# Attention with chunk selection and a gated MLP on one core: the k operands copied straight out of PSUM

## The chip, the core and the metric

The kernel runs on one core of a Trainium2 chip. The metric is the device time of one execution in microseconds (us). TensorE (PE in the profile), VectorE (DVE), ScalarE (ACT), GpSimd (POOL) and SyncE (SP) each work through an instruction list of their own, in order. DMA queues move data; here GpSimd issues the loads and SyncE the transposing transfers, the stores and, in the kernel before, some copies from one place of SBUF to another.

## What is computed

Attention for 4 batches of 8 heads with 768 tokens and 64 numbers to a head. A query sees its own and earlier tokens, and only those in the 6 best of 24 chunks of 32 keys; a chunk's worth is bounded from the minimum and the maximum of its keys. A gated MLP over the heads' joined output follows.

```python
def _attn_ref(q, k, v):
    k_chunks = k.reshape(B, H, nc, chunk, D)
    k_min = np.min(k_chunks, axis=3)
    k_max = np.max(k_chunks, axis=3)
    ub = np.sum(np.maximum(q[:, :, :, None, :] * k_min[:, :, None, :, :],
                           q[:, :, :, None, :] * k_max[:, :, None, :, :]), axis=-1)
    ub = np.where(causal, ub, -1000000000.0)
    top_chunks = np.argsort(ub, axis=-1)[..., -top_k:]
    scores = scale * np.matmul(q, k.transpose(0, 1, 3, 2))
    mask = sel & (pos[:, None] >= pos[None, :])
    scores = np.where(mask, scores, -1000000000.0)
    attn = softmax(scores)
    return np.matmul(attn, v)

def _moe_ref(x, w_in, w_spatial, b_spatial, w_out):
    h = np.maximum(x @ w_in, 0.0)
    u, v = (h[..., :d_ff // 2], h[..., d_ff // 2:])
    v_n = (v - mean(v)) / np.sqrt(var(v) + 1e-06)
    v_s = np.einsum('ts,bsd->btd', w_spatial, v_n) + b_spatial[None, :, None]
    return (u * v_s) @ w_out
```

## The kernel before

**Tiling.** The 32 heads are taken as 16 pairs, numbered 0 to 15, four to a batch. The two heads of a pair lie side by side on the 128 partitions (64 each). All matmul operands are f16. The MLP of a batch (v, u, s and o matmuls, in six blocks of 128 tokens) can begin when the four pairs of that batch are done, and is woven between the attention of later pairs.

**A pair.** `kT` transposes k on TensorE into one PSUM buffer of the pool `ps_ml` (L680), which has three buffers and is shared with every matmul of the MLP. VectorE reads that buffer twice, for `kmax` and `kmin` (L704), and forms the chunk bounds `kb`. `qT`, `rq` and `ub` give the bounds of each query, `top` and `sel` mark the chunks left out, and `aT`/`ac` (pairs 1 to 7) or the transposing transfer `aTd` (pairs 8 to 15, L826) make the other operand, a, of the scores. The stationary operand of the scores, `kh`, is one SBUF tile for each head, in a ring of four pairs: 64 of its partitions hold the chunk indicators (written once), and the other 64 hold the head's k. The step `kop` writes those 64 partitions, which lie in the opposite half to where they stand in the transposed k. Then `sc` multiplies (three PSUM buffers), ScalarE takes the exponential (`ex`, L842), `tri` on GpSimd cuts the diagonal, `av` accumulates in the single PSUM buffer `acc` (L859), `rc` and `nm` (L869) normalise out of it, and `x` brings the result across for the MLP.

**How kop is done.** For pairs 0 to 7 VectorE or ScalarE copies each half out of PSUM (L740). For pairs 8 to 15 there are three steps: one copy `kc` of the whole transposed k into SBUF by VectorE or ScalarE (L726), which together with the two reductions releases the PSUM buffer, and two transfers on SyncE's queue from that copy into `kh` (L738).

**Order.** Nothing is scheduled by the framework. A planner written in Python (`build`, `Sim`) searched an order beforehand, and the result stands in the file as the string `ORDER`, which names every step; each engine works through its own steps in that order. `PLAN` holds the parameters. Those that count here: `kcp` is the first pair whose k is copied to SBUF first, `flip` names the steps that go to the other engine of VectorE and ScalarE than the default, and `dum` is the number of dummy matmuls (`dm0` and on) that stand between the first steps. The rule in the planner and the step in the kernel:

```python
kd=i>=p['kdma']; kc=not kd and i>=p['kcp']
...
if (kd or kc) and p['kcdma'] and i>=p['kdm']:
    op(f'kop{i}{hi}','SP',.5,deps=[kt],acq=[('kh',i)],uses=[kr],...)
else:
    ke='ACT' if i<2 else 'DVE'
...
dst, src = self.kh[hi][d0:d1], getattr(self, "kTb", self.kT)[s0:s1]
if engine == "SP":
    nc.sync.dma_start(out=dst, in_=src)
else:
    copier(engine)(dst, src)
```

Of the kernel before, what the change touches and what calls it, by code (L numbers as in the profile page):

```python
# [390 lines left out]
PLAN = {'late': 40, 'mlp_first': 8, 'qbuf': 5, 'kbuf': 6, 'vbuf': 6, 'dum': 64, 'warm0': 5.3, 'kcp': 8, 'flip': ['ac10', 'ac41', 'ac51', 'ac60', 'ac71', 'gd34', 'kc10', 'kc12', 'kc13', 'kc9', 'kh00', 'kh11', 'kop00', 'kop40', 'kop71', 'oc01', 'oc03', 'oc13', 'oc21'], 'gp': ((3, 4), (3, 5)), 'lm': 0.2, 'lm2': 1.2, 'tm': 0.8, 'dum0': 42, 'split': 1, 'rpool': (4,), 'ract': (1,)}  # L391

ORDER = """
dz id0 dm ring3 lk010 ring2 ring1 lk000 ring0 lq010 small id1 lq000 expand lk001 kh00 kh30 kh11 lk011 kT0 kh21 mlat
dm0 kTb0 lq011 kmin0 dm1 dm2 dm3 dm4 dm5 kop01 dm6 dm7 dm8 dm9 dm10 dm11 lq001 kmax0 qTb0 kh31 qT0 dm12 lk11 dm13 dm14
dm15 dm16 kb0 dm17 dm18 dm19 rq00 dm20 rq01 dm21 dm22 dm23 dm24 dm25 dm26 kop00 dm27 dm28 dm29 dm30 lk10 kh20 kT1 ub0
kmax1 kTb1 kh01 lv0 dm31 dm32 dm33 dm34 dm35 dm36 dm37 dm38 dm39 top00 dm40 dm41 kop11 dm42 qT1 kmin1 lq10 dm43 dm44
dm45 kop10 dm46 dm47 dm48 dm49 dm50 dm51 dm52 dm53 selA0 dm54 top01 kh10 mtri aTA00 dm55 kb1 dm56 dm57 dm58 sel0 rq11
lq11 aTB0 dm59 rq10 dm60 dm61 dm62 dm63 acA00 ub1 wsp0 acB0 sc000 top10 win00 sc001 ex000 aTA01 top11 sc002 lk20 ex001
acA01 sc005 kT2 sel1 ex002 sc004 kop20 lk21 ex005 sc013 ex004 sc011 kmin2 ex013 aT10 lq20 sc003 ex011 sc010 ac10 av000  # L400
ex003 kop21 aT11 lq21 ex010 sc015 av001 sc100 kmax2 ex015 av002 ac11 lv1 sc012 rc00 kb2 ex012 qT2 nm00 sc102 ex100
rq21 kT3 lk31 ex102 av010 rq20 sc014 kmax3 sc112 ex014 win21 ub2 sc101 ex112 kmin3 win11 sc104 qT3 ex101 sc111 top20
av011 ex104 sc105 av012 kb3 lk30 ex111 top21 sc103 rc01 ex105 sel2 sc113 ex103 rq31 aT20 ex113 rq30 sc115 wsp4 sc114
ac20 nm01 ub3 kop30 av100 ex114 sc201 top30 av101 ex115 win01 ex201 sc203 kop31 av102 sc110 ex203 top31 aT21 ex110
rc10 lv2 sel3 kT4 ac21 nm10 qT4 sc200 kmin4 sc205 sc202 ex200 aT30 kmax4 ex202 sc215 av110 ex205 ex215 av111 rq40
kop40 sc211 wsp5 av112 kb4 rq41 sc204 sc212 ex211 rc11 kop41 ub4 aT31 ac30 sc210 top40 lq30 kT5 ex204 nm11 xp0 ex212
top41 lq31 av200 kop50 ac31 sc213 av201 sel4 ex210 av202 win30 sc214 kmax5 qT5 ex213 sc300 ex214 xp1 rc20 win20 rq51
sc301 ex300 sc310 nm20 ex301 rq50 av210 win31 ex310 kmin5 sc311 av211 sc303 ex311 win10 sc302 x1 av212 ex303 sc304
kop51 aT40 ex302 rc21 ex304 kb5 kT6 nm21 sc305 ac40 sc315 sc313 kmin6 av300 ex305 aT41 ex315 ex313 x0 sc404 wsp1 sc312
ac41 ex404 sc314 av301 kmax6 ex312 ub5 lk40 sc401 ex314 av302 sc400 top50 xp2 ex401 rc30 sc403 top51 ex400 sc402 wsp2  # L410
sel5 ex403 nm30 aT50 ring4 ex402 sc415 kop61 av310 ac50 av311 x2 sc412 ex415 av312 kop60 sc405 qT6 ex412 lq40 sc411
ex405 kT7 rc31 ex411 nm31 sc501 sc413 tri40 rq61 ex501 sc414 xp3 rq60 ex413 kmax7 wsp3 aT51 ex414 av400 sc502 kb6
sc410 kop71 x3 sc500 av401 ac51 v00.0 ex410 kmin7 av402 ex502 v00.2 tri41 ub6 ex500 kop70 sc504 sc503 lq41 sc505 top60
ex503 v02.0 top61 v04.0 ex504 lk41 rc40 v02.2 sel6 va00 nm40 sc510 qT7 va02 lk51 v04.2 ex510 rq71 sc513 kb7 av410 rq70
ex513 lq61 v01.0 bs02 av411 ex505 aT60 va04 bs00 v01.2 tri50 av412 ac60 sc514 va01 v03.0 lv3 rc41 vs02 nm41 sc603 ub7
ex603 bs01 v03.2 x4 sc511 ex514 lb top70 wsT0 ex511 av500 vs01 top71 sc512 lv4 va03 sc515 av501 sel7 wsT1 ex515 wsc0
sc600 ex512 av502 vs00 aT61 wsc1 ex600 v05.0 lq50 rc50 ac61 nm50 kT8 sc601 v05.2 kmax8 lq51 ex601 aT70 va05 sc604
kmin8 av510 lk61 ac70 sc613 sc602 u01.0 kc8 ex604 tri51 qT8 bs05 ex613 av511 wsT2 lk50 ex602 kb8 u01.2 rq80 sc611 rq81
u00.0 ex611 bs03 sc610 aT71 ua01 wsc2 av512 u00.2 ex610 vs05 bs04 sc704 wsT5 ua00 u02.0 vs04 ex704 ac71 wsT4 vs03 rc51
u02.2 rs0 nm51 sc605 sc614 wsc5 ub8 ex605 x5 ex614 sc612 wsc4 tri60 av600 ua02 sc700 vn00 av601 wsT3 ex612 vn04 sc701  # L420
ex700 u04.0 top80 av602 wsc3 sc703 u03.0 vn01 ex703 sc615 u04.2 rc60 ex701 nm60 u03.2 ua04 u05.0 top81 ua03 av610 sel8
sc702 vn03 ex615 sc710 aTd8 kT9 ex702 vn02 tri61 sc712 ex710 av611 kmin9 s00.0 lk60 ex712 u05.2 kop80 kmax9 av612
kop81 sc715 sc705 ua05 s00.2 wout1 rc61 ex715 qT9 vn05 kc9 sc711 s01.0 nm61 ex705 sc714 kop91 kb9 s00.4 rq91 tri70 x6
av700 rq90 s01.2 gt00 sc713 s02.0 ex713 gd00 av701 ub9 ex714 kT10 top90 s01.4 ex711 kop90 s02.2 top91 tri71 sc802 sel9
sc800 gt01 sc801 ex802 aTd9 av702 wout3 s02.4 ex801 rc70 wout2 s03.0 nm70 ex800 sc804 gt02 qT10 ex804 av710 kmax10
gd01 sc803 sc805 av711 sc810 ex803 s04.0 kmin10 ex805 av712 ex810 gd02 sc815 s03.2 tri80 ex815 rc71 sc812 kb10 kc10
nm71 s03.4 wout0 s04.2 ex812 x7 gt03 lv7 kT11 sc813 rq100 av800 ex813 sc811 rq101 gd03 av801 s05.0 kmax11 ex811 sc814
av802 s05.2 ex814 kop101 rc80 kmin11 s04.4 sc905 sc901 ub10 ex905 nm80 ex901 sc904 s05.4 kb11 gt04 ex904 sc900 av810
ex900 kc11 sc911 sc903 o01.0 ex911 top100 sc915 o00.0 top101 ex915 ex903 sc902 sel10 av811 o01.2 ex902 gt05 aTd10 qT11
sc910 oc01 tri90 v10.0 rq110 o00.2 tri81 kop100 rq111 sc914 v10.2 oc00 gd04 v11.0 lq60 ex914 ub11 ex910 av812 v11.2  # L430
gd05 lv5 va10 rc81 o02.0 nm81 va11 v13.0 top110 o02.2 kop110 top111 lq71 v14.0 sel11 oc02 sc912 bs10 av900 ex912 sc913
kT12 ex913 aTd11 v13.2 kmax12 v14.2 tri91 va13 av901 sc1000 kmin12 va14 sc1002 lk71 av902 ex1000 sc1012 v12.0 rc90
ex1002 nm90 o03.0 lk70 ex1012 bs11 sc1004 sc1005 av910 ex1004 bs14 qT12 av911 ex1005 o03.2 kc12 vs14 vs11 v12.2 oc03
sc1010 kop121 v15.0 va12 rq121 x8 av912 sc1003 sc1001 rc91 bs12 u10.0 ex1001 v15.2 rq120 os02 ex1010 u11.0 nm91 kop120
va15 u10.2 vs10 kop111 bs13 av1000 ua10 u11.2 os01 bs15 o04.0 ex1003 x9 kb12 kT13 ua11 vs13 tri100 o04.2 kmax13 sc1015
sc1014 oc04 sc1013 av1001 ub12 vs12 ex1014 kmin13 av1002 o05.0 ex1015 ex1013 sc1101 top120 u12.0 kc13 vs15 sc1011
rc100 top121 sc1104 ex1101 o05.2 kop130 sel12 ex1011 u13.0 nm100 os00 qT13 ex1104 kop131 tri101 u12.2 rq131 rs1 sc1100
aTd12 av1010 oc05 lv6 vn10 sc1103 sc1102 ua12 vn11 u13.2 ex1103 vn13 av1011 u14.0 ua13 vn14 u15.0 ex1100 rq130 av1012
u14.2 kb13 ex1102 rc101 vn15 u15.2 ua14 vn12 s10.0 ua15 sc1114 ub13 s10.2 top130 sc1110 sc1105 s10.4 nm101 ex1105
ex1110 s11.0 tri110 gt10 kT14 ex1114 s11.2 kmin14 lq70 gd10 s12.0 av1100 kmax14 sc1115 s11.4 ex1115 s12.2 gt11 sc1113  # L440
av1101 s12.4 kc14 gd11 sc1112 s14.0 gt12 ex1112 sc1111 av1102 top131 ex1113 s13.0 gd12 rc110 sel13 ex1111 s15.0 nm110
s14.2 tri111 sc1203 aTd13 sc1200 s14.4 ex1203 av1110 ex1200 gt14 s13.2 x10 av1111 sc1213 av1112 sc1201 ex1213 kT15
rc111 nm111 sc1202 s13.4 kmax15 ex1202 x11 sc1205 s15.2 ex1201 qT14 gt13 s15.4 ex1205 sc1215 kc15 sc1204 o10.0 ex1204
rq140 sc1210 kop151 av1200 gt15 ex1215 o10.2 os05 tri120 av1201 kb14 os03 rq141 sc1212 oc10 sc1302 kmin15 o12.0 gd13
ex1210 av1202 ex1212 ub14 rc120 sc1300 nm120 o12.2 gd15 ex1300 top140 sc1214 v21.0 ex1302 top141 v20.0 oc12 sel14
sc1310 ex1214 v21.2 sc1211 ex1310 qT15 sc1313 aTd14 ex1211 sc1303 rq150 v20.2 va21 rq151 tri121 av1210 ex1313 kb15
o11.0 gd14 ex1303 ub15 v23.0 va20 top150 av1211 sc1314 kop150 top151 sc1311 av1212 ex1314 bs20 o11.2 kop140 ex1311
# [21 lines left out]
def kernel(  # L469
# [20 lines left out]
    prm = dict(DEF)  # L490
    prm.update(PLAN)

# [395 lines left out]

    engine = {o.name: o.eng for o in build(PLAN).order}

# [201 lines left out]
```

## Time and profile before

| what | value |
|---|---|
| median of 4 runs | 204.28 us (202.27 to 205.67) |
| profiled execution, its own time | 202.27 us |
| its span, first to last instruction | 200.6 us |
| TensorE busy | 190.6 us (95%) |
| VectorE busy | 157.4 us (78%) |
| ScalarE busy | 149.0 us (74%) |
| GpSimd busy | 80.8 us (40%) |
| data moved by DMA | 28.60 MB |
| transfers kh<-kT | 16 of 96.0 KB |
| granted TensorE clock | 1.000 |

The profiled execution is one of the four runs, the fastest. Its span leaves out 1.67 us that lie around it (202.27 less 200.6), and it stands 2.01 us under the median. A matmul's busy time in the profile runs from its start to its modelled end, and matmuls overlap, so a busy TensorE is read from the spacing of matmuls rather than from the sum of their durations.

### The profile page before, as it was taken

Reading aid. Unit: us, or ns where it says so; the run is one execution under the profiler, and the core shown is the slowest. Engines: PE = TensorE matmul, PEld = TensorE weight load, DVE = VectorE, ACT = ScalarE, POOL = GpSimd, SP = SyncE. Lnnn points to the kernel's source line nnn. Section 1 sums busy time; section 2 is a strip of 40 time slices with the busy share of each in tenths; the row PEclk is TensorE's granted clock in tenths of the full one; section 3 lists DMA queues with packets and bytes.
Section 4 is the critical chain, followed back from the end, with each engine's and each line's share of the span. In section 5 each row is a group of like instructions: output and inputs, shape, how many; then the busy total and the mean of one; then the engine's idle time right before and its main releaser. Section 6 shows DMA issues by size and latency. Waiting matters only on the chain.

```text
span 200.6 us, 5309 instructions
## 1 busy us (share of the span) xinstructions
PE 190.6 (95%) x2057; PEld 120.9 (60%) x2057; DVE 157.4 (78%) x475; ACT 149.0 (74%) x296; POOL 80.8 (40%) x97
## 2 busy tenths in 40 slices
PE   7789789999999999999999999999999999999992
PEld 7777668767677756565566555656555555444451
DVE  6899799999999999899698899797378337257430
ACT  5969799999989986777888963689899751664151
POOL 7999957452899233453751412011212130000000
PEclk9999999999999999999999999999999999999999
DMA  6999999999699999999999999988672265342335
GB/s 40 98 122 163 164 161 182 170 194 82 64 141 135 151 122 164 175 166 159 140 140 164 235 180 161 182 215 116 211 120 39 78 121 149 115 179 85 78 128 212
DMA packets 114761, 28.60 MB, mean 143 GB/s; under 512 B 108720, under 2 KB 111280, under 8 KB 114736
## 3 DMA queue, kind: packets, MB, share of 16 engines
q0 software_dynamic: 76544, 12.20, 91.2%
q1 hardware_dynamic: 38192, 16.06, 40.6%
q8 instruction: 16, 0.26, 0.6%
q14 instruction: 9, 0.07, 0.1%
HBM read 24.38 MB, written 6.29 MB: 153 GB/s over the span
## 4 chain that ended last, share of the span: by engine, by line
PE 65%; DVE 12%; DMA 11%; POOL 6%; ACT 2%; issue 2%; SPq 1%; POOLq 0%; DVEq 0%; ACTq 0%
PE mlp L957 38%; PE sc L833 12%; PE acc L859 7%; DMA xT<-x 4%; DMA qs<-in_q_dram 3%; DMA kh<-kT 2%; DVE vn L994 2%; DVE kmm L704 2%; POOL k L619 2%; PE trq L745 2%; PE tra L820 1%; POOL qs L619 1%; DVE max L775 1%; DVE x L869 1%; PE kTp L680 1%
## 5 line engine op out<-in xcount | busy, mean ns | idle before, releaser
L842 ACT ACTIVATE e<-sc 128x512 f16<-128x512 f32 (+1 forms) x192 | 93.8, 561 | 20.0 <-PE sc L833 16.3
L833 PE MATMUL sc<-a,kh 128*128 128x512 f16 (+3 forms) x256 | 61.2, 305 | 0.6 <-DMA kh<-kT 0.3
L957 PE MATMUL mlp<-w_in_sb,xT 128*128 128x512 f16 x192 | 52.2, 379 | 0.0
L848 POOL TENSOR_SCALAR_AFFINE_SELECT e<-e 128x768 f16<-128x768 f16 x24 | 21.0, 877 | 75.9 <-ACT e L842 64.6
L859 PEld LDWEIGHTS <-e 128*128 128x128 f16 x672 | 31.4, 97 | 14.8 <-DVE x L869 0.9
L957 PE MATMUL mlp<-vn,wsT 128*128 128x512 f16 x144 | 38.8, 379 | 0.4 <-DVE vn L994 0.4
L859 PE MATMUL acc<-vt,e 128*128 128x65 f16 x672 | 35.8, 193 | 0.1
L704 DVE TENSOR_REDUCE kmm<-kTp 128x24 f16<-128x768 f16 x32 | 29.7, 948 | 1.9 <-PE kTp L680 1.9
L833 PEld LDWEIGHTS <-kh 128*128 128x128 f16 x256 | 22.6, 97 | 12.8 <-DMA kh<-kT 0.8
L957 PE MATMUL mlp<-w_out_sb,gT 128*128 128x512 f16 x92 | 26.1, 379 | 0.0
L957 PEld LDWEIGHTS <-xT 128*128 128x128 f16 x192 | 17.2, 97 | 14.4 <-issue 0.2
L1000 DVE SCALAR_TENSOR_TENSOR g<-mlp,b_col,u 128x512 f16<-128x512 f32 x24 | 17.9, 747 | 9.4 <-PE mlp L957 7.4
L1020 ACT COPY o<-mlp 128x512 f32<-128x512 f32 x19 | 11.1, 589 | 16.9 <-PE mlp L957 16.5
L979 DVE BATCH_NORM_STATS2 stats<-vraw 128x6 f32<-128x512 f32 x24 | 15.9, 678 | 5.8 <-ACT vraw L974 5.8
L957 PEld LDWEIGHTS <-wsT 128*128 128x128 f16 x144 | 12.7, 97 | 10.6 <-issue 0.4
L869 DVE TENSOR_TENSOR x<-acc,rec 128x384 f16<-128x384 f32 x32 | 17.7, 552 | 1.3 <-DMA xT<-x 0.8
L989 ACT ACTIVATE u<-mlp 128x512 f16<-128x512 f32 x24 | 14.0, 597 | 4.8 <-PE mlp L957 4.1
L775 DVE MAX8 max<-ub 128x8 f32<-128x8 f32 (+4 forms) x160 | 15.3, 167 | 1.0 <-PE ub L765 1.0
L974 ACT ACTIVATE vraw<-mlp 128x512 f32<-128x512 f32 x24 | 14.1, 606 | 2.4 <-PE mlp L957 2.4
L604 POOL DMA_DIRECT2D k<-in_k_dram x14 | 14.6, 1053 | 0.5 <-DMA ws_raw<-in_moe_w_spatial_dram 0.4
L610 POOL DMA_DIRECT2D qs<-in_q_dram x14 | 14.5, 1045 | 0.7 <-DMA k<-in_k_dram 0.7
L994 DVE TENSOR_SCALAR vn<-vraw,mv,rstd 128x512 f16<-128x512 f32 x24 | 13.7, 627 | 0.8 <-ACT rstd L1030 0.6
(85 smaller groups left out, 234.1 us busy)
## 6 DMA issues: line engine op xcount, KB each, us to landing
out_dram<-o SPq DMA_DIRECT2D x23, 256.0 KB, 2.3
vt<-in_v_dram POOLq DMA_DIRECT2D x8, 384.0 KB, 9.8
k<-in_k_dram POOLq DMA_DIRECT2D x14, 192.0 KB, 7.6
qs<-in_q_dram POOLq DMA_DIRECT2D x14, 192.0 KB, 7.7
kh<-kT SPq DMA_DIRECT2D x16, 96.0 KB, 4.9
ws_raw<-in_moe_w_spatial_dram POOLq DMA_DIRECT2D x6, 192.0 KB, 6.7
w_in_sb<-in_moe_w_in_dram POOLq DMA_DIRECT2D x8, 128.0 KB, 8.5
w_out_sb<-in_moe_w_out_dram POOLq DMA_DIRECT2D x4, 128.0 KB, 3.7
```

What stands on the lines that cost most here:

```text
L604: nc.gpsimd.dma_start(out=k_tile(g)[:, :, :, hi, :].rearrange("p x t d -> p (x t) d"), in_=source(k, b, 2 * hp + 2 * hi, 2))
L704: nc.vector.tensor_reduce(self.kmm[:, m, :], src, axis=AX.X, op=op, negate=(m == 1))
L775: nc.vector.max(self.max8[:, qi - 1, hi, :], self.ub[:, c0:c0 + CPT * (qi + 1)])
L833: mm(sc[:, col:col + n], lhsT=self.kh[hi][:, t * P:(t + 1) * P], rhs=self.a[:, q0 // P:(q0 + n) // P, hi, :], start=True, stop=not diag)
L842: nc.scalar.activation(out=self.e[hi][:, g * 512:g * 512 + width], in_=self.sc[hi, g][:, 0:width], func=Act.Exp, scale=scale)
L848: nc.gpsimd.affine_select(out=blk, in_=blk, compare_op=Alu.is_ge, fill=0.0, base=0, channel_multiplier=-1, pattern=[[0, NQT], [1, P]])
L859: mm(self.av[hi][:, qi, :], lhsT=self.e[hi][:, c:c + P], rhs=self.v[hi][:, t, 0:D + 1], start=first and n == 0, stop=last and n == len(blo ...
L869: nc.vector.tensor_tensor(self.x16[:, :, hi, :], in0=self.av[hi][:, :, 0:D], in1=self.rec[hi].to_broadcast([P, NQT, D]), op=Alu.mult)
L957: mm(st[kind, ti], lhsT=lhsT, rhs=rhs, start=(j == 0), stop=(j == n - 1))
L979: nc.vector.bn_stats(st["stats", ti], st["vraw"][:, ti, :])
L994: nc.vector.tensor_scalar(vn[:, ti, :], in0=st["vraw"][:, ti, :], scalar1=st["mv"][:, ti, 0:1], scalar2=st["rstd"][:, ti, :], op0=Alu.subt ...
L1000: nc.vector.scalar_tensor_tensor(g, in0=st["s", ti], scalar=b_col[:, ti:ti + 1], in1=st["u"][:, ti, :], op0=Alu.add, op1=Alu.mult)
```

## The change

`kcp` goes from 8 to 99, so no pair has a `kc` step any more. The two `kop` steps of pairs 8 to 15 are the copies that pairs 0 to 7 had already: 64 partitions by 768 numbers out of the PSUM buffer of the transposed k into `kh`, on VectorE or ScalarE. The tile kT in SBUF, its eight copies and the sixteen transfers on SyncE's queue are gone. The PSUM buffer of a pair's transposed k is then released by four readers, two reductions and two copies, in place of three. The order was searched anew, with another `flip` list, and 50 dummy matmuls in place of 64. All other functions of the kernel are as they were.

```diff
-PLAN = {..., 'dum': 64, 'warm0': 5.3, 'kcp': 8, 'flip': ['ac10', 'ac41', 'ac51', 'ac60', 'ac71', 'gd34', 'kc10', 'kc12', 'kc13', 'kc9', 'kh00', 'kh11', 'kop00', 'kop40', 'kop71', 'oc01', 'oc03', 'oc13', 'oc21'], ...}
+PLAN = {..., 'dum': 50, 'warm0': 5.3, 'kcp': 99, 'flip': ['ac11', 'ac20', 'ac31', 'ac40', 'ac41', 'ac51', 'ac70', 'ac71', 'kc10', 'kc11', 'kc8', 'kc9', 'kh01', 'kh21', 'kh31', 'kop100', 'kop101', 'kop110', 'kop111', 'kop120', 'kop141', 'kop150', 'kop31', 'kop40', 'kop50', 'kop51', 'kop71', 'kop81', 'kop90', 'kop91', 'oc10', 'oc11', 'oc12', 'oc13', 'oc14', 'oc15'], ...}
 ORDER = """
-dz id0 dm ring3 lk010 ring2 ring1 lk000 ring0 lq010 small id1 lq000 expand lk001 kh00 kh30 kh11 lk011 kT0 kh21 mlat
-dm0 kTb0 lq011 kmin0 dm1 dm2 dm3 dm4 dm5 kop01 dm6 dm7 dm8 dm9 dm10 dm11 lq001 kmax0 qTb0 kh31 qT0 dm12 lk11 dm13 dm14
...
-lq11 aTB0 dm59 rq10 dm60 dm61 dm62 dm63 acA00 ub1 wsp0 acB0 sc000 top10 win00 sc001 ex000 aTA01 top11 sc002 lk20 ex001
-acA01 sc005 kT2 sel1 ex002 sc004 kop20 lk21 ex005 sc013 ex004 sc011 kmin2 ex013 aT10 lq20 sc003 ex011 sc010 ac10 av000
...
-u02.2 rs0 nm51 sc605 sc614 wsc5 ub8 ex605 x5 ex614 sc612 wsc4 tri60 av600 ua02 sc700 vn00 av601 wsT3 ex612 vn04 sc701
...
-kop81 sc715 sc705 ua05 s00.2 wout1 rc61 ex715 qT9 vn05 kc9 sc711 s01.0 nm61 ex705 sc714 kop91 kb9 s00.4 rq91 tri70 x6
...
+dz id0 dm small lk000 ring2 ring1 lk010 ring0 lq000 ring3 id1 lq010 expand lk011 kh01 kh00 kh31 lk001 kT0 kh11 lq011
+dm0 kTb0 kh30 kmin0 dm1 dm2 dm3 dm4 dm5 dm6 lq001 dm7 dm8 dm9 dm10 dm11 kop00 kmax0 qTb0 mlat qT0 dm12 lk10 dm13 rq01
...
+acA01 lb sc001 top10 sc005 kT2 ex001 sc002 win00 top11 ex005 sc004 sel1 ex002 win30 sc013 kmax2 aT10 ex004 lk21 sc010
...
+sc604 u01.2 ex704 rq80 sc703 ex604 rc51 kb8 aT71 nm51 sc700 ex703 sc614 tri60 ac71 av600 rs0 sc702 kop80 av601 ua01
+ub8 av602 vn04 ex700 wsT2 rc60 ex614 nm60 sc701 wsT4 ex702 top80 tri61 av610 ex701 sc713 top81 sc712 kop81 av611 lk60
...
+ex715 kT9 ua03 tri71 u05.2 kmin9 s00.0 ua05 av701 s00.2 kmax9 s01.0 s00.4 rq91 kop90 s01.2 kb9 gt00 ub9 kop91 s01.4
+top90 gd00 av702 sc801 top91 sc802 sc805 ex801 s02.0 rc70 sel9 kT10 ex802 gt01 aTd9 sc800 ex805 s02.2 nm70 ex800 sc810
...
```

How many steps of each kind stand on an engine, before and after (kinds that do not change are left out):

| step | engine | before | after |
|---|---|---|---|
| kc, whole k to SBUF | VectorE / ScalarE | 4 / 4 | 0 / 0 |
| kop, pairs 8 to 15 | VectorE / ScalarE / SyncE | 0 / 0 / 16 | 6 / 10 / 0 |
| kop, pairs 0 to 7 | VectorE / ScalarE | 11 / 5 | 7 / 9 |
| ac, copy of a | VectorE / ScalarE | 5 / 9 | 8 / 6 |
| oc, copy of the output | VectorE / ScalarE | 4 / 20 | 6 / 18 |
| gd34, copy of the gate | VectorE / ScalarE | 0 / 1 | 1 / 0 |
| kh, indicators | VectorE / ScalarE | 2 / 6 | 3 / 5 |
| dm0 and on, dummy matmuls | TensorE | 64 | 50 |

## The prediction

> **What bounds the kernel now.** I read the busy time by stage first, then the waits, then the rows of the operations that the change removes or adds. I cut the stages where the work changes: 50.4 us is the first v matmul of the MLP, and 193.7 us the end of the o matmuls.
>
> ```profile
> core 0: us, PE busy (x) PEld busy (x) DVE busy (x) ACT busy (x) POOL busy (x), PEclk, DMA share, GB/s
> 0.00:50.40 50.40, 45.06 (x683) 36.45 (x684) 46.43 (x157) 44.30 (x81) 36.71 (x50) 1.00 1.73 138
> 50.40:75.00 24.60, 24.60 (x308) 16.76 (x307) 23.96 (x81) 22.31 (x47) 16.51 (x17) 1.00 2.06 121
> 75.00:120.00 45.00, 44.29 (x467) 26.55 (x466) 39.66 (x122) 34.94 (x73) 18.45 (x21) 1.00 1.69 169
> 120.00:165.00 45.00, 44.95 (x432) 25.89 (x429) 30.83 (x85) 33.81 (x72) 9.11 (x11) 1.00 0.82 140
> 165.00:193.70 28.70, 28.70 (x160) 13.55 (x157) 15.64 (x31) 11.27 (x22) 0.00 (x0) 1.00 0.39 120
> ```
>
> From 50.4 us on TensorE has 0.76 us without work in 143.3 (0.71 and 0.05). Its busy time counts modelled ends, so I set it against spacings. The chain of waits has the last MLP block back to back:
>
> ```profile
> 169.01 22.48 PE mlp L957 x104
> ```
>
> That is 0.216 us for a 512-column matmul. The timeline gives 0.056 for a 128-column transposition (six from 21.73 to 22.06), 0.030 for a matmul into acc and 0.025 for one into ub. Counting the steps behind the first v matmul with these gives 144.0 us of TensorE work, where 143.3 passed. So this part is TensorE's own work, end to end. Before it TensorE has dummies, and the pace is VectorE's and ScalarE's: from 10 us to 50.4 VectorE is idle 1.77 us, of which 1.2 us are one wait for a q load:
>
> ```profile
> 21.18 0.44 PE L745 MATMUL trq<-identity,qs 128*128 128x128 f16 x5 [1.27 <-DMA qs<-in_q_dram]
> 21.74 0.49 DVE L756 TENSOR_SCALAR rq<-trq 128x640 f16<-128x640 f16 x1 [1.20 <-PE trq L745]
> ```
>
> The waits between 50 and 194 us, where the changed steps lie (engine, waited for, us in total, times, longest):
>
> ```profile
> PEld L859 <- DVE x L869: 0.9, 2, 0.6
> PEld L833 <- DMA kh<-kT: 0.8, 1, 0.8
> ...
> ACT e L842 <- PE sc L833: 16.0, 26, 1.6
> ...
> ACT kT L726 <- DVE kmm L704: 0.6, 1, 0.6
> ```
>
> One wait of TensorE in that whole stretch is for a transfer of k. ScalarE is the one that waits: 16.0 us for scores.
>
> **The change part by part.** The rows that price it, of the groups and of the issues:
>
> ```profile
> L740 DVE COPY kh<-kTp 64x768 f16<-64x768 f16 x10 | 5.6, 555 | 0.3
> ...
> L726 ACT COPY kT<-kTp 128x768 f16<-128x768 f16 x4 | 3.2, 808 | 0.6 <-DVE kmm L704 0.6
> ...
> L726 DVE COPY kT<-kTp 128x768 f16<-128x768 f16 x4 | 2.2, 548 | 0.0
> ...
> L740 ACT COPY kh<-kTp 64x768 f16<-64x768 f16 x2 | 1.6, 794 | 0.3 <-DVE kmm L704 0.2
> ...
> kh<-kT SPq DMA_DIRECT2D x16, 96.0 KB, 4.9
> ```
>
> A copy of 64 partitions costs what one of 128 does. So one copy becomes two, not two halves.
>
> *VectorE*: 4 kc gone (-2.2), 6 kop for pairs 8 to 15 (+3.3), 4 kop of earlier pairs given to ScalarE (-2.2), 3 ac (542 ns each, +1.6), 2 oc (689, +1.4), gd34 (425, +0.4), one kh (676, +0.7): +3.0 us. *ScalarE*: 4 kc gone (-3.2), 14 kop (794, +11.1), 3 ac (837, -2.5), 2 oc (589, -1.2), gd34 (586, -0.6), one kh (828, -0.8): +2.8 us. Neither is the bound after 50.4 us, and ScalarE's 2.8 us are covered by its 16.0 us of waiting for scores. If that cover were gone, they would come onto TensorE in full.
>
> *Up to 50.4 us.* The same loads stand before the q load of pairs 2 and 3 in both orders (eight first ones, two of k, one of v), so it lands near 21.1 us again and both orders start from there together: what the head gains or loses before it is swallowed. From that point to the first v matmul VectorE has 32.1 us of work at mean durations in the old order and 32.1 in the new; ScalarE 31.0 and 30.9. The exchange of four kop for three ac cancels. I take 0, with -1.2 (the q wait gone) and +1 as ends. The 14 dummies less fill waits: 0. The load of v for pairs 4 and 5 is moved behind four more w_in loads and the q loads of pairs 6 and 7, less one w_spatial load: 4 x 128 + 384 - 192 = 704 KB more. From 28.0 to 36.3 us GpSimd issued 1,472 KB, 177 KB a us, so it goes 4 us later, at 32 us, and lands by 43.3 (longest landing of such a load: 11.3 us). Its first reader stands just ahead of the first v matmul, near 50: covered by some 7 us.
>
> *50.4 to 75 us.* VectorE is 97% busy. From the first v matmul to the last normalise of pair 7 the old order has 38.8 us of VectorE work for 34.1 of TensorE, the new one 38.4 for 33.4; scaled to the same TensorE work that is 0.4 us more. VectorE's late results reach TensorE here (the 0.9 us above are matmuls into acc that wait for a normalise, as acc is one buffer). I take +0.4, between 0 and 0.9.
>
> *The transfers.* The wait of 0.8 us on the weight load is one of 0.3 on TensorE's matmuls: about -0.4, between -0.3 and -1.1 (both rows added). It goes because the new copies stand early: from a kop to the first score that reads it there are 9.8 us of TensorE work or more from pair 8 on, where the transfers had 3.8 to 27.2 and took 4.9, at worst 7.7. SyncE loses 16 issues of 590 ns (9.4 us). Behind them in its queue stand aTd, x and gd; aTd has 7.0 us or more of TensorE work before its reader against a median landing of 5.7, and no row shows TensorE waiting for it: 0. The 1.5 MB less traffic is 5% of 28.6: 0.
>
> *The PSUM buffer and its readers.* This is the part the trace shows least. The row first: a copy on ScalarE out of the k buffer waited for VectorE's reduction 0.6 us once for kc and 0.2 once for kop, 0.8 us over six such instructions, 0.13 each. The Trainium skill, "PSUM — Partial Sum Buffer", section "PSUM bank collisions raise a hardware error", says that any two engines must be kept apart on a bank, reads against reads included; that speaks against sharing one k buffer between ScalarE and VectorE. In the new order 11 ScalarE copies wait on VectorE, 5 more. By the rule alone each could wait out both reductions (2 x 948 ns, 1.9 us), 9.5 us more on ScalarE, and the sum below would be up to 9.5 higher (about 214 us) wherever its waiting for scores does not cover them; by the row it is 0.7 us, inside that cover, and adds nothing. I take the row: most of these copies are written behind the reductions. Three VectorE reductions also wait for ScalarE (one before), at most 794 ns each: +1.6 us at most on VectorE after 120 us or near 40, where one case is inside the full stage; I take 0.3. The buffer itself is one of three that the MLP lives on. Between its transposition and its reuse the orders hold 4.2 to 6.5 us of TensorE work before (pairs 8 to 15), 4.6 to 7.6 after, and the last reader is written 1.2 us or more ahead of the reuse: I take +0.2, between 0 and the second rival's price.
>
> Sum: 0 + 0.4 - 0.4 + 0.3 + 0.2 = +0.5 us on the profiled 202.27, so 202.8. The median of the runs is 2.0 above the profiled execution; carried over, 204.8. Some of that scatter should be transfers landing late, and 16 fewer can do so; I take 0.5 off for it and forecast **204.3 us**.
>
> **The rivals.** *Faster: the runs' scatter was the transfers.* If the 2.0 us of the median are late k transfers (landings from 2.2 to 7.7 us against 3.8 us of cover at the tightest), the new kernel runs like the profiled execution, without the kh waits (-1.1) and without the q wait (-1.2): 200.0 us, 2.1% under the median. For it: the spread of 3.4 us over four runs. Against: one wait in the trace, and TensorE's work behind 50.4 us (144.0 against 143.8 in the new order) leaves nothing more to take.
>
> *Slower: the k copies stand in front of the evictions.* ScalarE and VectorE work in order. Behind a k copy stand exponentials, which free the three score buffers, and the evictions of the MLP, which free `ps_ml`, where the k buffer takes one of three. Place: 75 to 165 us. Price: if each of the 16 copies holds TensorE for its length, 10 x 0.79 + 6 x 0.555 = 11.3 us, less the kc's 5.4: +5.9 us, 210.2 by the median. It decides from 4.1 us on (2% of 204.28), so when seven tenths of these copies reach TensorE. For it: TensorE has no gap to hide anything, VectorE is 88% busy in 75 to 120. Against: ScalarE's 16.0 us, and the eight kc that held the same engines without a wait of TensorE.
>
> *The change isn't made*: excluded, since in the new instruction lists no kc and no k transfer is left.
>
> **How the numbers follow.** A measurement of this kernel tells about 2% from no change; its four runs spread 1.7%. No change within 2% (200.2 to 208.4): 0.52. Slower by the second rival, or by a part of it together with a poorer fit of a newly searched order in the stage where VectorE and ScalarE are full, which takes some 4 us of new stalls where TensorE has none today: 0.38. Faster: 0.10. The likeliest case alone runs from 201.5 (the lower ends, -1.2 and -1.1, and the 0.5 of scatter) to 206.5 (the upper ends of the two stages, the reductions' 0.3 and half a microsecond at the buffer, less the 0.3). The range goes from 200.8 to 209.5: below it stay most of the faster rival, above it the full second rival.
>
> **What would show it.** Right: the waits list has no kh transfer; TensorE from the first v matmul to the end of the o matmuls takes 143 to 145 us; the first v matmul is near 50 us; ScalarE still waits over 10 us for scores. Wrong towards slower: TensorE idle of over 2 us in 75 to 165 us, with mlp or sc matmuls waiting for ScalarE or VectorE. Wrong towards faster: the first v matmul before 49 us. If that point moves later by over 1 us, the argument from the q load is wrong.

## The result and the profile after

The changed kernel took **204.37 us** (median of 43 runs, 202.80 to 205.91), the kernel before 203.43 us beside it (64 runs, 201.07 to 206.52). The ratio is **1.0064, interval 1.0046 to 1.0081**: slower by 0.64%, or 1.3 us, and within 2%. The ratio compares fast runs alone, without those over 1.5% above the fastest of their kernel, of which the kernel before has more; over all runs the medians differ by 0.94 us. The forecast was 204.3 us, with "within 2%" as the likeliest case.

The profiled execution of the changed kernel has its own time at 205.05 us, 0.7 above its median; that of the kernel before was 1.2 below its median. So the two traces differ by 2.7 us of span (203.3 against 200.6), where the runs differ by 1.3.

The stages of the changed kernel, in the columns of the table by stage shown above (length, busy time of each engine with its instructions, granted clock, DMA share, GB/s):

```profile
10.00:50.40 40.40, 36.26 (x558) 28.29 (x556) 38.06 (x132) 36.78 (x73) 31.63 (x40) 1.00 1.93 159
50.40:75.00 24.60, 24.21 (x314) 16.64 (x313) 23.29 (x80) 23.39 (x49) 15.44 (x16) 1.00 1.63 108
75.00:120.00 45.00, 42.99 (x461) 25.97 (x459) 37.91 (x123) 37.11 (x75) 16.85 (x18) 1.00 1.67 142
120.00:165.00 45.00, 45.00 (x417) 25.69 (x416) 34.72 (x90) 31.95 (x66) 7.49 (x9) 1.00 0.58 133
165.00:193.70 28.70, 28.70 (x163) 13.72 (x162) 15.22 (x31) 12.79 (x25) 0.86 (x1) 1.00 0.36 91
```

TensorE is without work for 0.39 us in 50.4 to 75 (before: none) and for 2.01 in 75 to 165 (before: 0.76). From 120 us on it has none. The first v matmul, the last output matmuls and the two longest idle times of 75 to 165 us, in the timeline of the kernel before and then of the changed one:

```profile
50.22 0.60 PE L957 MATMUL mlp<-w_in_sb,xT 128*128 128x512 f16 x2
...
195.66 0.59 PE L957 MATMUL mlp<-w_out_sb,gT 128*128 128x512 f16 x2
196.09 0.60 PE L1041 MATMUL mlp<-w_out_sb,gT 128*128 128x256 f16 x4
```

```profile
22.04 0.72 PE L744 MATMUL trq<-identity,qs 128*128 128x128 f16 x10 [1.60 <-DMA qs<-in_q_dram]
...
50.83 0.59 PE L956 MATMUL mlp<-w_in_sb,xT 128*128 128x512 f16 x2
...
94.82 0.59 PE L956 MATMUL mlp<-w_in_sb,xT 128*128 128x512 f16 x2
96.62 0.59 PE L956 MATMUL mlp<-w_out_sb,gT 128*128 128x512 f16 x2 [1.21 <-DVE g L999]
...
104.68 0.38 PE L832 MATMUL sc<-a,kh 128*128 128x384 f16 x2
105.60 0.60 PE L956 MATMUL mlp<-w_out_sb,gT 128*128 128x512 f16 x2 [0.54 <-DMA gT<-g]
...
198.37 0.59 PE L956 MATMUL mlp<-w_out_sb,gT 128*128 128x512 f16 x2
```

The q load of pairs 2 and 3 landed 0.86 us later (22.04 against 21.18), and the first v matmul stands 0.61 us later: 28.79 us behind the first transposition of that q, where it was 29.04. The last matmul of 512 columns into the output starts at 198.37 us, against 195.66 before. So the 2.71 us of the pair of traces are 0.61 at the head and 2.10 between these two matmuls (147.54 us against 145.44); the idle time above holds 1.64 of the 2.10. Most of the other 0.46 us belongs to the same waits: the profile counts a wait from the modelled end of the matmul before it, and for 512 columns that end lies 0.16 us behind the point where the next one could start (0.38 us of duration against 0.216 of spacing). By the spacing, the wait ahead of 96.62 us cost 1.37 us (96.62 less 94.82, less two matmuls of 0.216), and the one ahead of 105.60 us cost 0.70. Both stand in front of o matmuls, and the list of waits says for what. For the changed kernel, 50 to 194 us (engine, waited for, us in total, times, longest):

```profile
ACT e L841 <- PE sc L832: 11.1, 18, 1.4
...
DVE g L999 <- DMA gT<-g: 3.3, 2, 2.4
...
PEld L956 <- DMA gT<-g: 1.7, 2, 0.8
...
PE mlp L956 <- DVE g L999: 1.2, 1, 1.2
ACT kh L739 <- DVE kmm L703: 0.8, 1, 0.8
...
PE mlp L956 <- DMA gT<-g: 0.5, 1, 0.5
PE wtr L648 <- DVE wsT L650: 0.4, 1, 0.4
```

No line of TensorE names `kh`. Its two longest waits both come from `gT`: the step `gd` on SyncE's queue (L1014) transposes a finished gate tile `g` into `gT`, which the o matmuls of the first batch read. The gate tiles have three buffers, so a late transfer also holds the next `g` on VectorE. The chain of waits shows the two transfers (start, length, what):

```profile
87.70 8.02 DMA gT<-g
...
95.81 0.75 DVE g L999
...
98.09 7.46 DMA gT<-g
...
105.60 0.60 PE mlp L956 x2
```

Over the whole run such a transfer takes 2.4 us in the median (3.0 in the kernel before); these two took 8.02 and 7.46. At the same time GpSimd issues loads in a row, as its timeline shows:

```profile
86.50 0.57 POOL L640 DMA_DIRECT2D w_out_sb<-in_moe_w_out_dram  x1
87.06 3.05 POOL L609 DMA_DIRECT2D qs<-in_q_dram  x3
90.07 1.06 POOL L603 DMA_DIRECT2D k<-in_k_dram  x1
91.08 1.46 POOL L614 DMA_DIRECT2D vt<-in_v_dram  x1
92.47 1.07 POOL L603 DMA_DIRECT2D k<-in_k_dram  x1
```

By the sizes of the issues (128, 3 x 192, 192, 384, 192 KB) these are 1,472 KB in 7 us. The kernel before is not free of such loads: from 85.8 to 98.7 us it issued 1,280 KB, and five `gT` transfers issued between 85 and 105 us took 7.2 us in the median (four of the changed kernel: 7.7). What differs is the room. Counted in TensorE work between the `gd` and the first o matmul that reads it (spacings of matmuls, in the order of the steps, that o step included), the old order leaves batch 0 8.3 to 14.6 us, the new one 7.2 to 14.2, and three of its six tiles lost most: 12.1 to 7.8, 14.6 to 7.2, 13.8 to 7.8. A transfer of 7.5 to 8 us no longer fits. A second trace of the changed kernel (the one of experiment 7) has the same kind of waits at other places, one for `gT` and one for an `x` that is held by the transfer of an earlier `x`:

```profile
PE acc L858 <- DVE x L868: 0.8, 1, 0.8
PE mlp L956 <- DMA gT<-g: 0.7, 1, 0.7
```

So what is late is the transposing transfers of this stretch, and which of them TensorE meets differs from one execution to the next.

### The profile page after: what moved, and what is told of

Same layout as the page of the kernel before. It is cut to its first block, busy times and chain, and to the rows that moved or that the text cites. A ratio compares the mean times of both kernels' runs of the same rounds, so it can differ in the third digit from the quotient of the medians.

```text
span 203.3 us, 5261 instructions
## 1 busy us (share of the span) xinstructions
PE 190.3 (94%) x2043; PEld 120.3 (59%) x2043; DVE 159.0 (78%) x480; ACT 152.9 (75%) x299; POOL 81.0 (40%) x97
## 4 chain that ended last, share of the span: by engine, by line
PE 63%; ACT 12%; DMA 11%; POOL 6%; DVE 3%; issue 2%; SPq 1%; POOLq 0%; DVEq 0%; ACTq 0%
PE mlp L956 40%; PE sc L832 11%; ACT e L841 9%; DMA gT<-g 8%; PE acc L858 6%; DMA qs<-in_q_dram 4%; POOL k L618 2%; PE kTp L679 1%; POOL qs L618 1%; PE trq L744 1%; ACT a L822 1%; PE ub L764 1%; ACT kh L739 1%; PE tra L819 1%; DVE vn L993 1%
## 5 line engine op out<-in xcount | busy, mean ns | idle before, releaser
L841 ACT ACTIVATE e<-sc 128x512 f16<-128x512 f32 (+1 forms) x192 | 93.0, 559 | 15.4 <-PE sc L832 11.1
L956 PE MATMUL mlp<-vn,wsT 128*128 128x512 f16 x144 | 38.3, 379 | 0.0
L988 ACT ACTIVATE u<-mlp 128x512 f16<-128x512 f32 x24 | 14.2, 599 | 9.1 <-PE mlp L956 8.4
L1019 ACT COPY o<-mlp 128x512 f32<-128x512 f32 x17 | 10.0, 586 | 13.3 <-PE mlp L956 13.2
```

Source lines behind the costliest of these rows:

```text
L841: nc.scalar.activation(out=self.e[hi][:, g * 512:g * 512 + width], in_=self.sc[hi, g][:, 0:width], func=Act.Exp, scale=scale)
L956: mm(st[kind, ti], lhsT=lhsT, rhs=rhs, start=(j == 0), stop=(j == n - 1))
```

## The experiments

Two theories stood against each other after the result. By one, the k copies cost nothing worth naming, and the 0.64% are the new order's: late gate transfers behind the loads of 86 to 93 us, and perhaps a later q load. By the other, the copies cost, as the second rival had it, and the new order hides most of it. Ratios are to the kernel before, run beside on the same chip.

**1. The old order with the new route.** Each `kc` of the old order is replaced in place by the two `kop` of its pair, on different engines for four of the eight pairs; nothing else of the order moves.

```diff
-'kcp': 8, 'flip': [..., 'kc10', 'kc12', 'kc13', 'kc9', ...]      ORDER: ... kc8 ...
+'kcp': 99, 'flip': [..., VectorE: 80 121 130 131 140 151, ScalarE: the other ten of pairs 8 to 15]      ORDER: ... kop80 kop81 ...
```

> The order of before with the new k route alone: each kc of pairs 8 to 15 is replaced where it stands by its two kop, on VectorE for 80, 121, 130, 131, 140, 151 and on ScalarE for the other ten; the 16 transfers are gone. Nothing else moves. Theory A (the new order costs, the route does not): ratio to before 0.995 to 1.002, no wait of TensorE on kh. Theory B (the copies out of PSUM cost, by holding VectorE, ScalarE and the shared buffer): 1.005 or more, with TensorE idle in 75 to 165 us behind ScalarE or VectorE.

Measured: 205.34 us, ratio **1.0156 (1.0093 to 1.022)**. The waits of its TensorE in the profile, all of them between 89 and 109 us:

```profile
PE mlp L957 <- ACT kh L740: 1.1, 1, 1.1
...
PE kTp L680 <- ACT kh L740: 0.5, 1, 0.5
PE mlp L957 <- DVE kh L740: 0.4, 1, 0.4
```

These are the second rival's waits: MLP matmuls and the next transposition of k held by a k copy, 2.0 us in all. The profiled execution is the slowest of the six (207.75 us), with a fall of the clock near 24 us that the last section shows. From the first v matmul on, where its clock is 1.00, to the last output matmul of 512 columns it takes 149.16 us, 3.7 more than before. By the spacing the three waits cost 2.5 of these; the rest is not told apart. The theory that the route is free in any order falls.

**2. The same with both copies on one engine.** As 1, but both copies of a pair stay where its `kc` was, so that no buffer is handed from one of the two engines to the other between them. In 1 the copies had waited for each other at such places:

```profile
ACT kh L740 <- DVE kh L740: 2.1, 2, 1.6
...
DVE kh L740 <- ACT kh L740: 1.4, 2, 0.9
```

```diff
-kop 80, 121, 130, 131, 140, 151 on VectorE, the other ten on ScalarE
+kop of pairs 9, 10, 12, 13 on ScalarE, of pairs 8, 11, 14, 15 on VectorE
```

> As the run of the old order with the new route, but both copies of a pair on the engine that its kc had (pairs 9, 10, 12, 13 on ScalarE, 8, 11, 14, 15 on VectorE), so no pair's buffer is handed from one engine to the other between its copies. That run lost 2.0 us of TensorE behind kh copies, and its ScalarE waited 2.1 us for VectorE's copy of the same buffer. If the handing over is the cost: ratio to before 1.005 to 1.010. If it is that each buffer is held for a second copy and the engines are full there: 1.012 to 1.020 again, with TensorE waiting for kh copies as before.

Measured: 205.45 us, ratio **1.0174 (1.0135 to 1.0214)**, no better than 1. Its waits in the profile:

```profile
PE mlp L957 <- ACT kh L740: 1.0, 2, 0.6
...
PE kTp L680 <- ACT kh L740: 0.5, 1, 0.5
```

The waits of the copies for each other are gone and the time is not shorter, so the handing between two engines is not the cost. What both runs have is a second copy where the engine had none; 1.5 us of the waits here carry its name, and from the first v matmul to the last output matmul this trace (clock 1.00 throughout) takes 148.97 us, 3.5 more than before. The rest of the 3.5 is not told apart here either.

**3. The new order with the old route.** The first `kop` of each pair from 8 on becomes the `kc` copy, and the two transfers go onto SyncE's queue.

```diff
-'kcp': 99      ORDER: ... kop80 ... kop81 ...
+'kcp': 8       ORDER: ... kc8 kop80 (SyncE) kop81 (SyncE) ...
```

> The new order with the old k route: in pairs 8 to 15 the first kop is replaced by a kc and the two transfers right behind it (kc 8, 11, 14, 15 on VectorE, the others on ScalarE). Theory A: the loss stays, ratio to before 1.004 to 1.012, with waits of VectorE and TensorE on gT near 95 to 106 us, if anything longer, as 16 transfers more stand in SyncE's queue. Theory B: the loss goes, 0.998 to 1.002.

Measured: 215.79 us, ratio **1.0672 (1.061 to 1.0733)**, by far the worst. The waits of the DMA queues' engine show why. SyncE works in order, and k transfers stand waiting for their copies, 22.2 us in four waits, with the transposing transfers of the MLP behind it:

```profile
SPq L738 <- ACT kT L726: 13.0, 2, 8.3
...
SPq L738 <- DVE kT L726: 9.2, 2, 8.7
```

And TensorE, from 50 to 200 us:

```profile
PE mlp L957 <- DVE g L1000: 3.0, 1, 3.0
...
PE acc L859 <- DVE x L869: 2.4, 1, 2.4
...
PE mlp L957 <- DMA gT<-g: 1.6, 1, 1.6
PE mlp L957 <- DMA xT<-x: 1.4, 1, 1.4
```

The new order leans on a queue that carries no k. Each mix is a searched order with steps replaced by hand, not one searched for its route. So order and route are fitted to each other: of the four combinations, each mixed one is slower than both pure ones (1.0156 and 1.0672 against 1 and 1.0064).

**4. Six gate tiles instead of three** in the changed kernel, which takes away VectorE's wait for the transfer of an earlier tile.

```diff
-g = st["g", ti] = ml.tile([P, DH], F16, tag="g", name="g", bufs=3)
+g = st["g", ti] = ml.tile([P, DH], F16, tag="g", name="g", bufs=6)
```

> The changed kernel with six buffers for the gate tile g in place of three, nothing else. In its profile VectorE waited 3.3 us for a gT transfer to free a g buffer, and TensorE 1.2 us behind that. Theory A1 (the loss is the late gT transfers, reaching TensorE through the g buffers): that wait of VectorE is gone, ratio to before 0.998 to 1.003. Theory A2 (late gT reaches TensorE through the o matmuls themselves) or C (the loss is at the head): stays 1.005 to 1.008.

Measured: 204.10 us, ratio 1.0061 (1.0031 to 1.009): no gain is seen. VectorE's wait is gone from the list, but the transposed a of the scores comes through the same queue, and its wait grew from 0.3 us to 1.2:

```profile
PE sc L832 <- DMA a<-qs: 1.2, 1, 1.2
```

The wait moved; the late transfers stayed.

**5. The load of the bias later.** `lb` (b_col, issued in the changed kernel at 15.24 us, between the q load that TensorE waits for and the next loads) goes to where `lv4` stands.

```diff
-... acA01 lb sc001 ...      ... wsT0 lv4 ...
+... acA01 sc001 ...         ... wsT0 lb lv4 ...
```

> The changed kernel with the load of the MLP's bias (lb, b_col, 768 numbers of 4 bytes) moved on GpSimd from right behind the q load of pairs 2 and 3 to just ahead of the v load of pairs 8 and 9, near where it was before. Theory C (the bias load delays that q load, which landed 0.85 us later than before): TensorE's first trq of pair 2 is back near 21.2 us from 22.04, the first v matmul near 50.2 from 50.83, ratio to before 1.002 to 1.004. Theory A: the head comes back or not, but the ratio stays 1.005 to 1.008.

Measured: 203.99 us, ratio 1.0062 (1.0037 to 1.0088). From its timeline and its stages:

```profile
20.53 0.72 PE L744 MATMUL trq<-identity,qs 128*128 128x128 f16 x10 [0.44 <-DMA qs<-in_q_dram]
```

```profile
75.00:120.00 45.00, 42.77 (x452) 25.53 (x451) 37.42 (x121) 37.22 (x75) 17.44 (x18) 1.00 1.70 145
```

In this trace the q load is there 1.5 us earlier and the first v matmul starts at 49.32 instead of 50.83, but the time is that of the changed kernel: TensorE is idle for 2.23 us in 75 to 120, behind late transposing transfers again (1.2 us for a of the scores, 0.8 for an `x`, 0.2 for `gT`). How much of the 1.5 us is the edit is doubtful. Over the profiles of all runs of the new order the first transposition of that q stands at 21.00 to 22.04 us with the bias load ahead (five, mean 21.4) and at 20.23 to 21.32 with it moved (five, mean 20.7), so the edit is worth some 0.7 us there, and the rest is scatter from one execution to the next.

**6. The loads of 86 to 93 us spread.** `lq60`, `lq61`, `lk61` and `lv5` go to where the GpSimd queue is empty, `lk70` and `lv7` behind the burst.

```diff
-... sel8 ... lv7 ... lq60 ... lq61 ... lk61 ... lv5 ... lk70 ... gd05 ...
+... wout1 lq60 lq61 ... lk60 lk61 lv5 sel8 ... gd05 lk70 ... tri110 lv7 ...
```

> The changed kernel with GpSimd's burst of loads at 86 to 93 us taken apart, nothing else: q and k of pairs 12 and 13 and v of pairs 10 and 11 are issued before 80 us, k of pairs 14 and 15 (second half) behind the gates of batch 0, v of pairs 14 and 15 near 125 us. Theory D (that burst makes the transposing transfers of gT and a late, up to 8 us, and TensorE loses some 2 us at 95 to 106 us behind them): TensorE idle under 0.8 us in 75 to 120 us (2.0 in the changed kernel), ratio to before 0.997 to 1.003. Theory E (the loss is spread: double copies on full engines, with the transfers only the place where slack shows): the waits at 95 to 106 go, the ratio stays at 1.004 to 1.008.

Measured: 202.98 us, ratio **1.0033 (1.0003 to 1.0063)**. The stage from 75 to 120 us, its stretch around the two idle times, and the gate transfers issued from 85 to 105 us:

```profile
75.00:120.00 45.00, 44.57 (x477) 26.89 (x475) 40.15 (x127) 38.45 (x77) 14.46 (x15) 1.00 1.24 130
95.00:106.00 11.00, 11.00 (x105) 6.24 (x104) 8.79 (x27) 9.20 (x20) 3.84 (x4) 1.00 0.37 73
```

```profile
gT<-g SPq DMA_TRANSPOSE x4, 2.4
```

The transfers are back at 2.4 us (7.7 in the changed kernel), and TensorE has no idle time from 95 to 106 us. This is the cause of the two waits, shown: the k copies are untouched here.

It brings only half of what these waits cost. From the first v matmul to the last output matmul the trace takes 146.49 us, 1.05 less than the 147.54 of the changed kernel, where the two waits had cost 2.07 by the spacing. What took their place are waits for VectorE, the first of which was 0.4 us before the edit and the second not in the list:

```profile
PE wtr L648 <- DVE wsT L650: 0.8, 1, 0.8
PE mlp L956 <- DVE vn L993: 0.4, 1, 0.4
```

Ahead of that copy `wsT` VectorE took 2.30 us for two `vn` steps, where it was 1.85, while GpSimd issued the loads that the edit had moved there. That is an overlap in time; the cause is not shown.

**7. Edits 4, 5 and 6 together**, and again on another chip beside the changed kernel.

> The changed kernel with the loads spread, the bias load late and six g buffers together. Theory D: the head gain of the late bias load (first w_in matmul 49.3 in place of 50.4 to 50.8) is no longer given back at 80 to 105 us: ratio to before 0.992 to 0.999, faster than both kernels. Theory E: 1.003 to 1.007.

> Loads spread, bias load late, six g buffers, again. Theory D: 0.997 to 1.002 to before and 0.4 to 0.8% under the changed kernel beside it. If it stands at the changed kernel's ratio here, the earlier gain was the chip's.

> The changed kernel itself, to stand on one chip beside the two that follow. 1.0046 to 1.0081 to before, as measured first.

Measured: 202.72 us, ratio **1.0010 (0.9991 to 1.0029)**, and again 202.69, **0.9993 (0.9969 to 1.0017)**; the changed kernel beside the second 204.32, 1.0074 (1.0048 to 1.01). The three edits are worth 1.6 us, 0.8%, and bring the new route level with the kernel before. Part of that is at the head: in the five traces of experiments 6 to 8 the first v matmul starts at 49.2 to 50.1 us (before: 50.22), and from there to the last output matmul they take 146.1 to 146.5 us against the 145.44 of the one trace of the kernel before. The old order with its loads spread was not run, so whether the two routes are level when both orders get this care is open. How the three edits share the gain is not told apart: 6 alone gave about half, and its interval meets that of all three.

**8. One more wait.** In 7 TensorE still waits 0.8 us for the copy `wsc3` on VectorE (the line for `wsT` under 6). It goes ahead of `vn02`.

```diff
-... ex711 vn02 ... ex705 wsc3 u04.2 ...
+... ex711 wsc3 vn02 ... ex705 u04.2 ...
```

> The changed kernel with the loads spread, the bias load late, six g buffers, and the copy wsc3 of a transposed w_spatial block moved on VectorE from behind the vn steps vn02 and vn00 to ahead of them. With the first three alone TensorE still waited 0.8 us near 74 us for that copy, which frees a buffer of ps_ml, and the ratio was 1.001. Theory D (what is left of the loss are single waits in the order): that wait goes, ratio to before 0.994 to 0.999. Theory E (the double copies hold the kernel back everywhere a little): the ratio stays 1.000 to 1.003, as the wait turns up elsewhere.

> The same with wsc3 early, again. If the copy was worth its 0.8 us: 0.3 to 0.4% under the run with the three edits. If the wait only moves: the same as that run within 0.15%.

Measured: 203.11 us, ratio 0.9973 (0.9945 to 1.0), and beside 7 on one chip 202.79, 1.0000 (0.9975 to 1.0025), against 0.9993 of 7. That wait is gone, and TensorE waits instead for `rq`, made from the transposed q:

```profile
PE ub L761 <- DVE rq L755: 0.6, 1, 0.6
```

The edit is worth nothing that these runs can tell, and no version is clearly faster than the kernel before.

## Why the prediction was right, and which step failed

The case that was held likeliest came in, and the number within 0.1 us. Two terms of the sum were off in opposite directions, so the closeness is partly luck.

*The base.* The median of four runs that the sum was carried to, 204.28, lies 0.85 us above that of the 64 runs (203.43). The change in the sum was +0.5 less 0.5 for the scatter, that is nothing; the medians over all runs make it +0.94 us and the ratio +1.3. So 0.85 too much and 0.94 too little met in the forecast.

*TensorE end to end.* A reading that was wrong. 193.7 us is where the chain that ended last leaves TensorE, not the end of the o matmuls: the last of them start at 195.66 and 196.09 us. The 144.0 us of work stand against some 146 us (50.65 to 196.5), not 143.3, so the old kernel had some 2 us to gain, of which 0.76 show as idle. Also, the upper ends of the likeliest case sum to 206.7, not 206.5. Neither changes the forecast.

*The end without k transfers.* Right: no line of TensorE names kh. What the wait was worth by itself no run isolates.

*Up to 50.4 us.* Right. The first v matmul follows the first transposition of that q by 29.0 us in both traces of the old order without a clock dip (the kernel before and experiment 2) and by 28.8 to 29.0 in all ten of the new one, so the q load sets it, as argued, and the work from there on is equal to 0.25 us. The +0.61 is the load's landing, which scatters by 1.0 us over five executions with the same loads ahead of it; the bias load behind it may have a part (experiment 5). The load of v for pairs 4 and 5 went at 35.7 us, not at 32, and nothing waited for it.

*50.4 to 75 us.* Right: 0.39 us of idle TensorE where +0.4 was taken, and it waits for a copy of VectorE (`wsT`).

*The copies' readers.* Right: ScalarE's copies waited 0.8 us for a reduction (the row made it 0.7 over eleven copies, the rule of the skill up to 9.5), and ScalarE still waits 11.1 us for scores. Experiment 2 supports it: with both copies on one engine the time stays where it was.

*The buffer's hold.* Right for this order, at no wait of TensorE. It is not free as such. In the old order the same copies brought 1.5 us of kh waits in the trace of experiment 2, 2.0 in that of experiment 1, and 1.6% more time. So the second rival's mechanism exists, at its place (86 to 114 us in these two traces), with a third of its price in waits that name it (2.0 of 5.9 us) and somewhat over half if the whole 1.6% (3.2 us) is put down to it, and the new search is what removes it.

*Transfers behind the k transfers, costed at 0.* **This is the step that failed.** The prediction looked at the room of aTd (7.0 us or more; 6.3 at the tightest, counted to the first score in the order) and named x and gd without counting any room for them. That "no row shows TensorE waiting for it" was read from the old order. The new order took 4 to 7 us off the room of three gate tiles, while the loads of 86 to 93 us kept their transfers at 7.5 to 8 us. It cost 1.2 and 0.5 us of TensorE's waiting in the trace, 2.07 us by the spacing of the matmuls, and experiment 6 removes it without touching a k copy. For aTd the room did not hold either: TensorE waited 0.3 us for one (1.2 in experiments 4 and 5), as its transfers took 7.1 us there. I had costed 16 fewer transfers on SyncE's queue as pure relief; what the queue gained in issue time it could not give to a transfer that is slow in the DMA itself.

*The scatter.* The runs do lie closer together (standard deviation 0.73 us against 1.30 before), and so the medians over all runs differ by 0.94 us where the ratio makes it 1.3: some 0.4 of the 0.5 us that were taken off. That the transfers of k made the scatter is not shown.

*The signs.* No kh wait, ScalarE's wait over 10 us and the first v matmul moved by less than 1 us spoke for the likeliest case. Two spoke against: TensorE took 2.1 us more from the first v matmul to the last output matmul, which is 145.4 by the prediction's measure (143.3 and 2.1), against 143 to 145; and TensorE's idle time in 75 to 165 us was 2.01, just over the bound, but behind gate transfers and not behind ScalarE's or VectorE's k copies. A sign that names only the idle time would have pointed at the wrong rival; the name of the wait decided.

## What to carry to other kernels

A change that comes with a new search is two changes: run the old order with the new route and the new order with the old route, since both mixes here were slower than either kernel. When an order moves, count the room of every consumer that is fed by a DMA, also of those that the edit does not name, and set it against the landing times under the loads of that stretch rather than against the median of the run. And before a wait is removed, look at what is late next in the same queue: here the edit that took a wait away (experiment 4) and the one that brought the first loads sooner (experiment 5) gained nothing that could be told alone.

## What the hardware showed that I had not expected

A transposing transfer that takes 2.4 us in the median took 7.5 to 8 us while GpSimd's queue was putting out 1,472 KB of loads in 7 us, and 2.4 us again with those loads spread. I had thought of the queue (SyncE's issues) as what delays such a transfer.

TensorE's clock fell behind a single wait. In experiment 1 it had worked 1.81 to 1.96 of every 2 us from 14 to 20 us, then waited 1.93 us for q; the stages of 2 us that follow (same columns as above) show the granted clock at 0.75, 0.50 and 0.90:

```profile
20.00:22.00 2.00, 0.27 (x5) 0.30 (x6) 0.46 (x1) 0.93 (x2) 1.85 (x3) 1.00 1.82 183
22.00:24.00 2.00, 2.00 (x30) 1.53 (x27) 1.71 (x4) 1.04 (x2) 1.99 (x3) 0.75 2.36 149
24.00:26.00 2.00, 2.00 (x23) 1.60 (x22) 1.89 (x13) 1.69 (x4) 1.60 (x2) 0.50 2.44 156
26.00:28.00 2.00, 2.00 (x31) 1.49 (x30) 0.90 (x4) 1.57 (x5) 0.52 (x1) 0.90 2.46 157
```

The changed kernel waited 1.60 us at the same place and kept 1.00. The Trainium skill, "TensorE: Matmul & The Clock Gate", "Part 1: The HAM clock gate", puts the fall behind an idle window of about 3.4 us; here it fell behind a wait of 1.93 us. In experiment 3, where TensorE was busy for 1.02 us of the 5 from 95 us on, the clock was 0.52 in the next 5, and the two 512-column matmuls that start at 102.75 us stand 0.85 us ahead of the next pair, where two take 0.43 at full clock. So in these traces a long wait was paid for a second time behind it.
